# Gating the row loads of batches 2 and 3 to the MLP passes, five value blocks by crossbar, and a new order for batch 0, in a chunked-attention and MLP kernel

## The chip, the cores and the metric

One core of a Trainium2 chip runs the whole kernel. The metric is device time of one execution in microseconds (us), the median of several runs; lower is better. A profile is one further execution, taken by the hardware profiler, in which every instruction has a start and a duration.

The engines named below: TensorE (PE; PEld is its weight load, which overlaps), VectorE (DVE), ScalarE (ACT), GpSimd (POOL) and SyncE (SP). POOL and SP issue nearly all DMAs here. [...]

## The reference

Four batches, eight heads, 768 positions of 64 numbers. Attention goes by chunks of 32 queries; each chunk sees its own 32 positions, 16 to the left, 8 to the right, and 8 memory positions of its batch and head. The result of all heads becomes rows of 512, and each row goes through an MLP with a sine in it.

```python
for c in range(S // 32):
    l_start, r_end = max(0, 32 * c - 16), min(S, 32 * c + 32 + 8)
    k_full = concat([mem_k, k[:, :, l_start:r_end]], axis=2)
    v_full = concat([mem_v, v[:, :, l_start:r_end]], axis=2)
    a = softmax(q[:, :, 32 * c:32 * c + 32] @ k_full.T / sqrt(64))
    attn[:, :, 32 * c:32 * c + 32] = a @ v_full
x = attn.transpose(0, 2, 1, 3).reshape(4 * 768, 512)
h = x @ w_in                      # 512 -> 2048
g = h + sin(alpha * h) ** 2 / (alpha + 1e-9)
out = g @ w_out                   # 2048 -> 512, float32
```

Keys, queries, values and weights are cast to bf16 on the way in; sums are float32.

## The kernel before

The work is cut by batch. A batch has an attention part, a first MLP pass (`layer`: 16 tiles `ft` of 128 hidden columns, each two halves of four 384-column matmuls, L483) and a second MLP pass (`second`: six row blocks `s`, each 16 matmuls of 512 columns, L529, then a copy out of PSUM to `o_sb` and a store). The second pass of a batch is put into a `Feed` and dealt out in small shares between the instructions of the next batch's attention and first pass. So PE's order, written by hand, is: attention 0, first pass 0, second pass 0 mixed with turning K and Q of batch 1 and with attention 1, first pass 1, then attention 2 mixed with second pass, and so on; last comes second pass 3 alone.

Attention works on eight blocks `j` of 96 queries with 128 keys each (16 left, 48, 8 memory, 48, 8 right). `scores` (L270) makes the transposed scores of all heads, ACT takes three exponentials (L283), `values` (L296) multiplies by V with a column of ones, DVE normalizes (L302, L303) into `x_blk`, and the block is turned into `xT`, the operand of the first pass. There are two ways to turn it: `turn_x` (four PE transposes, L313, and a DVE copy, L316), or a crossbar DMA issued on SP (L467). The argument `crossed` of `attention` says how many of the eight blocks take the crossbar: 0 in batches 1 and 2, 5 in batch 3. `ahead` begins the first pass of a batch inside its attention, as soon as half of `xT` is there.

K and Q come in two ways. Batches 0 and 1 load them with many positions per partition (`load_qk`), and PE turns them (`turn`); for batch 1 POOL first puts two heads side by side (`pair_up`). Batches 2 and 3 load rows (`load_rows`, 22 POOL DMAs with rows of 64 numbers: 16 for `kst`, 6 for `qst`), and SP turns them by crossbar DMA into `kTs` and `qTs` (`cross_steps`, 14 DMAs). The rows of batch 2 are issued before attention 1, their crossings partly beside attention 1, the rest at tile 0 of first pass 1. The rows of batch 3 are issued at the end of first pass 1, and all 14 crossings come at tile 2 of first pass 2.

V is loaded by `load_v` into `vws` (two buffers, one for even and one for odd batches): per block 48 + 48 rows in the middle, and two more DMAs for the edges of 16 and 8 rows. Memory values go in by a DVE copy for batch 0 (`put_memv`) and by eight SP DMAs for the others (`send_memv`). V of batch 1 is issued at tile 11 of first pass 0, V of batches 2 and 3 after attention 1 and 2.

Each POOL or SP queue works in order, and a DMA's issue waits on its queue until its semaphores allow it. POOL's DMAs share eight completion semaphores in turn, so that the ninth waits for the first to land; SP's have eight as well. All stores of `o_sb` are on SP, with the crossings. `o_sb` has two buffers. In a first pass an even row block is copied out by DVE (L542) and an odd one by ACT (L544); in an attention (`state["attending"]`) all are copied by ACT.

Batch 0 has its own attention, by head pair `hp` and half: `unit_scores`, `unit_values`, `unit_turn`. PE's order in `attention_first` has dummy matmuls in it (`warm`, L323). All scores come first, then the eight `pv` (values) and `x` (turn) units.

PSUM banks are handed out from rings set by `plan`: `one` (single banks: turned blocks, second pass, warm), `big` (pairs: scores, values, the first pass begun ahead), `h` (pairs of the first pass), `t` (turned K and Q).

Of the kernel before, what the change touches and what calls it, by code (L numbers as in the profile page):

```python
# [42 lines left out]
def kernel(  # L43
# [37 lines left out]
    def plan(**sets):  # L81
        for kind, ring in sets.items():
            rings[kind] = list(ring)
# [37 lines left out]
    memkT = consts.tile([P, HP, 32], BF, name="memkT")  # L121
    w_in_sb = consts.tile([P, KT, d_ff], BF, name="w_in_sb")
    w_out_sb = consts.tile([P, FT, d_model], BF, name="w_out_sb")
    ident_f = consts.tile([FT, FT], F32, name="ident_f")
    alpha_sb = consts.tile([P, FT], F32, name="alpha_sb")
    inv_alpha = consts.tile([P, FT], F32, name="inv_alpha")
# [3 lines left out]
    def alloc_qk():  # L130
        kb = qkst.tile([P, H, 6, D], BF, name="k_bf")
        qb = qkst.tile([P, H, 6, D], BF, name="q_bf")
        return kb, qb

    def load_rows(b):
        for j in range(NJ):
            lo = QW * j - 16
            r0 = max(0, -lo)
            nc.gpsimd.dma_start(  # L139
                kst[r0:64, j, :].rearrange("p (h d) -> p h d", d=D),  # L140
                k[b, :, lo + r0:lo + 64, :].rearrange("h p d -> p h d"),
            )
            n = min(56, S - (QW * j + 48))
            nc.gpsimd.dma_start(  # L144
                kst[72:72 + n, j, :].rearrange("p (h d) -> p h d", d=D),
                k[b, :, QW * j + 48:QW * j + 48 + n, :].rearrange("h p d -> p h d"),
            )
        nc.sync.dma_start(
            kst[64:72], memk_st[64:72, b - 2, :].unsqueeze(1).to_broadcast([NM, NJ, H * D])
        )  # L150
        for t in range(NSUB):
            nc.gpsimd.dma_start(  # L152
                qst[:, t, :].rearrange("p (h d) -> p h d", d=D),
                q[b, :, P * t:P * t + P, :].rearrange("h p d -> p h d"),
            )

    def cross_steps(b):
        for j in range(NJ):
            nc.sync.dma_start_transpose(kTs[b % 2][:, :, P * j:P * j + P], kst[:, j, :])
            yield  # L160
        for t in range(NSUB):
            nc.sync.dma_start_transpose(qTs[b % 2][:, :, P * t:P * t + P], qst[:, t, :])  # L162
            yield

    def load_qk(b, bufs, h0, h1):
        for src, dst in ((k, bufs[0]), (q, bufs[1])):
# [4 lines left out]

    def load_v(b, parts=((0, H),)):
        vw = vws[b % 2][:].rearrange("p h j c -> p (h j) c")
        vf = v[b].rearrange("h (j t) d -> t (h j) d", t=QW)
        n = H * NJ
        if len(parts) > 1:
            load_v_edges(vw, vf, n)
        for h0, h1 in parts:
            c0, c1 = h0 * NJ, h1 * NJ
            nc.gpsimd.dma_start(vw[16:64, c0:c1, 0:D], vf[0:48, c0:c1])  # L180
            nc.gpsimd.dma_start(vw[72:120, c0:c1, 0:D], vf[48:96, c0:c1])
        if len(parts) == 1:
            load_v_edges(vw, vf, n)

    def load_v_edges(vw, vf, n):
        nc.gpsimd.dma_start(vw[0:16, 1:n, 0:D], vf[80:96, 0:n - 1])
        nc.gpsimd.dma_start(vw[120:128, 0:n - 1, 0:D], vf[0:8, 1:n])

    def put_memv(b, eng, h0, h1):
        eng.tensor_copy(  # L190
# [188 lines left out]
    def attention_first(kq, alphas, ahead):  # L379
# [3 lines left out]
        def turn_k(hp):  # L383
            t = turn(kq[0], hp, None)
            put_k(0, hp, t)
            put_k_edges(0, hp, t)

        def turn_q(hp):
            put_q(0, hp, turn(kq[1], hp, None))

        def sc(hp):
            for half in range(2):
                pt[hp, half] = unit_scores(hp, half)

        def pv(*u):
            xb[u] = unit_values(*u, pt[u])
# [11 lines left out]
        put_memk(0)  # L408
        warm(3)
        turn_k(1)  # L410
        warm(2)
        sc(0)
        turn_q(1)
        alphas()
        put_memv(0, nc.vector, 0, H)
        warm(2)
        turn_k(2)
        warm(2)
        sc(1)
        turn_q(2)  # L420
        turn_k(3)
        warm(4)
        turn_q(3)
        sc(2)
        warm(2)
        sc(3)
        nc.scalar.preload_act_table(ACTF.Sin)
        send_memv(1)
        plan(big=(4, 0, 2), one=(6, 7))
        units = [(hp, half) for hp in range(HP - 1) for half in range(2)]  # L430
        pv(0, 0)
        for n in range(1, len(units)):
            warm(1)
            pv(*units[n])
            warm(1)
            x(*units[n - 1])
        warm(1)
        pv(3, 0)
        x(2, 1)
# [80 lines left out]
    def second(i, gT, cut=0):  # L520
# [15 lines left out]
        def end_o(s, bank):  # L536
            kept.remove(bank)
            rings["one"].remove(bank)
            rings["one"].append(bank)
            o_sb = mlp.tile([P, d_model], F32, name="o_sb", bufs=2)  # L540
            if s % 2 == 0 and not state["attending"]:
                nc.vector.tensor_copy(o_sb[:], ps[:, bank, :])  # L542
            else:
                nc.scalar.copy(o_sb[:], ps[:, bank, :])  # L544
            nc.sync.dma_start(out[S * i + P * s:S * i + P * s + P, :], o_sb[:])
# [26 lines left out]
        nc.vector.memset(vw[96:128, H - 1, NJ - 1, 0:D], 0.0)  # L572
    load_qk(0, kq, 0, 2)
    masks.make_identity(nc, ident[:])
    for hp in range(1, HP):
        load_qk(0, kq, 2 * hp, 2 * hp + 2)
    load_v(0, [(2 * hp, 2 * hp + 2) for hp in range(HP)])
    nc.gpsimd.dma_start(memv_st[64:72, 1:B].rearrange("n b h d -> n (b h) d"),
                        mem_v[1:B].rearrange("b h n d -> n (b h) d"))
    for kT in kTs:  # L580
        nc.vector.memset(kT[:, :, 0:16], 0.0)
        nc.vector.memset(kT[:, :, 848:856], 0.0)
# [37 lines left out]
    xT = attention_first(kq, alphas, ahead)  # L620
    for c in range(2):
        load_w_out(c)
    kq1 = alloc_qk()
    load_qk(1, kq1, 0, H)
    for bb in range(2):
# [29 lines left out]
    def begin_0(ft):  # L655
        if ft == 3:
            plan(h=[6] + rings["big"])
        if ft == 11:
            load_v(1)
        if ft == 15:  # L660
            prs.extend(pair_up(kq1[0], n) for n in range(3))

    layer(0, xT, "VPPAPAVPPAPAVAAA", begin_0, 0)
    last4 = rings["h"]
# [2 lines left out]
    feed.take(20)  # L667
    for pc in range(2 * HP):
        hp = pc % HP
        if pc + 3 < 2 * HP:  # L670
            prs.append(pair_up(kq1[(pc + 3) // HP], (pc + 3) % HP))
        t = turn(None, hp, prs[pc])
        if pc < HP:
            put_k(1, hp, t)
            put_k_edges(1, hp, t)
        else:
            put_q(1, hp, t, hp % 2 == 1)
        feed.take(2)
    nc.scalar.preload_act_table(ACTF.Exp)
    feed.take(4)  # L680
    load_rows(2)
    crossings = cross_steps(2)
    xT = attention(1, feed, (6, 8, 4, 4, 4, 3, 3, 3, 3, 1, 1), 2, 0, crossings, 3)
    load_v(2)
    send_memv(2)

    for i in range(1, B):
        last = i == B - 1
        if i > 1:
            crossings = cross_steps(i + 1) if not last else iter(())  # L690

        def begin(ft, i=i):
            if ft == (2 if i > 1 else 0):
                for _ in crossings:
                    pass

        if i == 1:
            assert feed.left() == 16
# [5 lines left out]
            plan(h=rings["big"])  # L704
            layer(i, xT, "AAAV", begin, feed.left() - (0 if last else 16))
        if not last:
            if i + 2 < B:
                load_rows(i + 2)
            plan(big=rings["h"])
            nc.scalar.preload_act_table(ACTF.Exp)  # L710
            feed.take(6)
            xT = attention(i + 1, feed, (4, 8, 4, 4, 3, 3, 3, 3, 4, 4, 4), 2, 5 if i == B - 2 else 0)
            if i + 2 < B:
                load_v(i + 2)
                send_memv(i + 2)
    feed.take(200)


# [28 lines left out]
```

The softmax here doesn't subtract the row's maximum and nothing guards it: scores larger than these inputs give would overflow.

## Time and profile before

Three runs took 225.8 to 226.97 us, the median is 226.94. The profiled execution took 227.97 us; its span from the first to the last instruction is 226.2 us, so 1.8 us lie around the span.

| Stage (us of the span) | What PE does |
|---|---|
| 0 to 5.6 | warm-up, while the first K lands |
| 5.6 to 29.1 | attention 0, and the first pass begun ahead |
| 29.1 to 49.2 | first pass 0 |
| 49.2 to 61.3 | K and Q of batch 1 turned, second pass 0 |
| 61.3 to 78.3 | attention 1 with second pass 0 |
| 78.3 to 99.7 | first pass 1 |
| 99.7 to 118.9 | attention 2 with second passes 0 and 1 |
| 118.9 to 149.7 | first pass 2 with second pass 1 |
| 149.7 to 168.0 | attention 3 with second passes 1 and 2 |
| 168.0 to 226.2 | first pass 3, second passes 2 and 3 |

Views used in this document: the page (busy time of each engine, DMA queues, groups by line), a table of stages, the waits of an engine, the chain of work that ended last, the timeline of an engine, and the DMA view of a stretch. In a row of a timeline stand the start, the duration, the engine, the line, the operation and the count; a bracket gives the idle time before it and who ended it.

### The profile page before, as it was taken

To read this page: it belongs to the slowest core of one execution; us is meant where nothing else is said; L and a number is where in the kernel's file an instruction comes from. 1 tells how busy PE (TensorE), PEld (TensorE's weight loads), DVE (VectorE), ACT (ScalarE), POOL (GpSimd) and SP (SyncE) were. 2 spreads that over 40 slices of the span, in tenths; PEclk is the share of its full clock that TensorE was granted. 3 is DMA by queue.
4 is the path that set the end of the run, shared out by engine and by line. 5 is a ranking of instruction groups with operands and counts; after the bars stand their busy time and mean duration, and the time that the engine had idled before them with its cause. 6 is when DMAs were issued, how large, how long until landed. Compare 5 with 4: busy or idle time off the path is not lost.

```text
span 226.2 us, 4432 instructions
## 1 busy us (share of the span) xinstructions
PE 212.5 (94%) x1694; PEld 115.9 (51%) x1720; DVE 132.9 (59%) x234; ACT 152.6 (67%) x226; POOL 84.4 (37%) x106
## 2 busy tenths in 40 slices
PE   7998999999998999999999999978999999999992
PEld 2555555555545655554665555534565555544440
DVE  5684748793516769994763875626653773771110
ACT  2558478894787589999756879777939678651011
POOL 8967843796989941185780000000000000000000
PEclk9999999999999999999999999999999999999999
DMA  5999999999999999999999954542330110111211
GB/s 81 174 121 127 157 210 207 206 204 142 103 216 159 142 112 167 117 135 121 151 180 95 96 95 93 96 139 93 73 110 0 49 46 0 48 48 49 93 65 74
DMA packets 94573, 25.97 MB, mean 115 GB/s; under 512 B 82632, under 2 KB 91480, under 8 KB 94552
## 3 DMA queue, kind: packets, MB, share of 16 engines
q0 software_dynamic: 71520, 14.81, 111.5%
q1 hardware_dynamic: 23032, 10.88, 24.5%
q8 instruction: 13, 0.21, 0.5%
q14 instruction: 8, 0.07, 0.1%
HBM read 29.67 MB, written 6.29 MB: 159 GB/s over the span
## 4 chain that ended last, share of the span: by engine, by line
PE 50%; DVE 7%; ACT 4%; SPq 3%; issue 3%; DMA 1%; DVEq 0%; ACTq 0%
PE ps L529 26%; PE ps L483 18%; DVE gT L513 5%; SPq L162 3%; PE ps L296 2%; PE ps L270 2%; DVE u L510 2%; ACT u L503 2%; PE ps L313 1%; ACT u L507 1%; DMA out_dram<-o_sb 1%; ACT o_sb L544 1%; ACT pt L283 0%; DVE o_sb L542 0%; DVEq L513 0%
## 5 line engine op out<-in xcount | busy, mean ns | idle before, releaser
L529 PE MATMUL ps<-w_out_sb,gT 128*128 128x512 bf16 x362 | 94.7, 379 | 1.5 <-ACT o_sb L544 0.4
L483 PE MATMUL ps<-xT,w_in_sb 128*128 128x384 bf16 x512 | 91.2, 326 | 1.6 <-DVE gT L513 1.2
L513 DVE SCALAR_TENSOR_TENSOR gT<-u,inv_alpha,ps 128x768 bf16<-128x768 f32 x64 | 63.3, 1011 | 24.0 <-ACT u L507 20.0
L483 PEld LDWEIGHTS <-w_in_sb 128*128 128x128 bf16 x512 | 49.6, 98 | 39.0 <-issue 3.4
L503 ACT ACTIVATE u<-ps,alpha_sb 128x768 f32<-128x768 f32 x64 | 56.7, 896 | 18.4 <-PE ps L483 17.5
L529 PEld LDWEIGHTS <-gT 128*128 128x128 bf16 x384 | 34.3, 98 | 30.9 <-issue 0.9
L507 ACT ACTIVATE u<-u 128x768 f32<-128x768 f32 x40 | 33.7, 843 | 1.2
L283 ACT ACTIVATE pt<-ps,biasm 128x256 bf16<-128x256 f32 x72 | 28.6, 481 | 6.7 <-PE ps L270 3.2
L544 ACT COPY o_sb<-ps 128x512 f32<-128x512 f32 x16 | 9.4, 589 | 25.5 <-PE ps L529 25.5
L510 DVE TENSOR_TENSOR u<-u 128x768 f32<-128x768 f32 x18 | 17.1, 953 | 6.0 <-ACT u L503 6.0
L542 DVE COPY o_sb<-ps 128x512 f32<-128x512 f32 x8 | 5.5, 690 | 21.8 <-PE ps L529 17.2
L303 DVE TENSOR_TENSOR x_blk<-ps,rinv 96x512 bf16<-96x512 f32 x24 | 16.5, 686 | 0.8
L144 POOL DMA_DIRECT2D kst<-in_k_dram x16 | 11.6, 725 | 8.8 <-DMA vw<-in_v_dram 4.1
L302 DVE RECIPROCAL rinv<-ps 96x8 f32<-96x8 f32 x24 | 4.9, 202 | 17.0 <-ACT pt L283 10.7
L139 POOL DMA_DIRECT2D kst<-in_k_dram x16 | 11.0, 689 | 8.6 <-DMA vw<-in_v_dram 6.2
L323 PE MATMUL ps<-idle 128*128 128x512 bf16 x35 | 12.5, 448 | 1.5 <-DVE vw L571 1.2
L249 ACT COPY kT<-ps 128x672 bf16<-128x672 bf16 x8 | 5.8, 719 | 9.5 <-PE ps L234 6.7
L296 PEld LDWEIGHTS <-pt 128*128 128x128 bf16 x192 | 9.0, 98 | 4.6 <-issue 0.7
L510 POOL TENSOR_TENSOR u<-u 128x768 f32<-128x768 f32 x6 | 8.9, 1495 | 6.1 <-ACT u L503 6.1
L152 POOL DMA_DIRECT2D qst<-in_q_dram x12 | 10.6, 899 | 1.2 <-DMA kst<-in_k_dram 1.2
L270 PE MATMUL ps<-qT,kT 64*128 64x96 bf16 x192 | 8.3, 205 | 2.6 <-DVE gT L513 2.3
L296 PE MATMUL ps<-vw,pt 128*128 128x65 bf16 x192 | 9.8, 193 | 0.4 <-issue 0.3
(77 smaller groups left out, 150.8 us busy)
## 6 DMA issues: line engine op xcount, KB each, us to landing
out_dram<-o_sb SPq DMA_DIRECT2D x24, 256.0 KB
vw<-in_v_dram POOLq DMA_DIRECT2D x6, 384.0 KB, 14.9
w_out_sb<-in_moe_w_out_dram POOLq DMA_DIRECT2D x2, 1024.0 KB, 18.8
w_in_sb<-in_moe_w_in_dram POOLq DMA_DIRECT2D x3, 512.0 KB, 10.1
qst<-in_q_dram POOLq DMA_DIRECT2D x12, 128.0 KB, 7.0
kst<-in_k_dram POOLq DMA_DIRECT2D x14, 64.0 KB, 6.7
kst<-in_k_dram POOLq DMA_DIRECT2D x14, 56.0 KB, 6.4
k_bf<-in_k_dram POOLq DMA_DIRECT2D x4, 192.0 KB, 4.7
```

What stands on the lines that cost most here:

```text
L270: nc.tensor.matmul(sc[:, e, QW * hp:QW * hp + QW], kTs[b % 2][64 * e:64 * e + 64, hp, pitch * j:pitch * j + P], qTs[b % 2][64 * e:64 * e + ...
L283: nc.scalar.activation(pt[:, 0:H * QW].rearrange("p (g e c) -> p g e c", g=2, e=4)[:, :, :, 32 * m:32 * m + 32], sc[:, :, 0:4 * QW].rearra ...
L296: nc.tensor.matmul(otv[:, e, hp, :], pt[:, QW * i:QW * i + P], vws[b % 2][:, 2 * hp + e, j, 0:D + 1],)
L303: nc.vector.tensor_tensor(out=x_blk[:].rearrange("p g e d -> p e g d"), in0=otv[0:QW, :, :, 0:D], in1=rinv[:].unsqueeze(3).to_broadcast([Q ...
L323: nc.tensor.matmul(z, idle[:, 0:P], idle[:])
L483: nc.tensor.matmul(hT[:, hf, 0:HALF], w_in_sb[:, kt, P * ft:P * ft + P], xT[:, kt, HALF * hf:HALF * hf + HALF], start=(kt == 0), stop=(kt ...
L503: nc.scalar.activation(u[:], hT[:, :, 0:HALF], ACTF.Sin, scale=alpha_sb[:, ft:ft + 1])
L507: nc.scalar.activation(u[:], u[:], ACTF.Square)
L510: eng.tensor_tensor(out=u[:], in0=u[:], in1=u[:], op=ALU.mult)
L513: nc.vector.scalar_tensor_tensor(out=gT[:, ft, :].rearrange("p (e c) -> p e c", e=2), in0=u[:], scalar=inv_alpha[:, ft:ft + 1], in1=hT[:, ...
L529: nc.tensor.matmul(ps[:, bank, :], gT[:, ft, P * s:P * s + P], w_out_sb[:, ft, :], start=(ft == 0), stop=(ft == FT - 1),)
L544: nc.scalar.copy(o_sb[:], ps[:, bank, :])
```

## The change

Six things are changed.

- **Row loads.** `load_rows` issues K and Q in the order in which the blocks need them (`order`), and the crossings take the same order. The rows of batch 2 are issued at tile 0 of first pass 1, those of batch 3 at tile 0 of first pass 2. Ahead of each set POOL copies one element of `xT`, the last that attention writes, into `gate`, so that the loads behind it on POOL start when that attention is over. The crossings of batch 2 are all issued at tile 0 of first pass 1, those of batch 3 one per tile from tile 1 of first pass 2.
- **V loads.** `load_v` takes the edges along: 64 + 56 rows per block in two DMAs. V of batches 1 and 2 and both `send_memv` go at tile 11 of first pass 0; V of batch 3 follows the rows of batch 3, `send_memv(3)` attention 2.
- **Crossbar.** Attention 1 and 2 send five value blocks through the crossbar, as attention 3 did already.
- **Copies out.** In an attention all `o_sb` copies go to DVE.
- **Batch 0.** V of the first head pair is issued ahead of K and Q of pairs 2 and 3; `put_memv` is earlier; three values units and two turns are placed between the scores. Eight dummy matmuls fewer are issued.
- **Batch 1.** Four head pairs are paired up at tile 15 instead of three, and later ones after the turn instead of before it. The memory values' load is behind the loads of `w_out`.

```diff
+    order = ((0, 0), (1, 1), (2, 2), (3,), (4, 3), (5, 4), (6, 5), (7,))
     def load_rows(b):
-        for j in range(NJ):
+        for jt in order:
+            j = jt[0]
...
+            for t in jt[1:]:
+                nc.gpsimd.dma_start(qst[:, t, :]..., q[b, :, P * t:P * t + P, :]...)
...
     def load_v(b, parts=((0, H),)):
...
+            if b == 0 and h0 == 0:
+                part(16, 64, 0, 0, 1)
+                c0 = 1
+            part(0, 64, -16, c0, c1)
...
+            part(72, 128, 48, c0, c1)
...
         turn_k(1)
+        put_memv(0, nc.vector, 0, H)
         warm(2)
         sc(0)
         turn_q(1)
         alphas()
-        put_memv(0, nc.vector, 0, H)
-        warm(2)
-        turn_k(2)
-        warm(2)
+        warm(3)
         sc(1)
+        t2 = turn(kq[0], 2, None)
+        put_k(0, 2, t2)
+        pv(0, 0)
+        put_k_edges(0, 2, t2)
         turn_q(2)
-        turn_k(3)
-        warm(4)
+        warm(1)
+        pv(0, 1)
+        t3 = turn(kq[0], 3, None)
+        put_k(0, 3, t3)
+        warm(1)
+        x(0, 0)
+        sc_half(2, 0)
+        put_k_edges(0, 3, t3)
         turn_q(3)
-        sc(2)
-        warm(2)
+        sc_half(2, 1)
+        x(0, 1)
+        warm(1)
+        plan(big=(4, 0, 2))
+        pv(1, 0)
         sc(3)
...
-            if s % 2 == 0 and not state["attending"]:
+            if s % 2 == 0 or state["attending"]:
...
         if ft == 11:
             load_v(1)
+            load_v(2)
+            send_memv(1)
+            send_memv(2)
...
-    load_rows(2)
-    crossings = cross_steps(2)
-    xT = attention(1, feed, (6, 8, 4, 4, 4, 3, 3, 3, 3, 1, 1), 2, 0, crossings, 3)
-    load_v(2)
-    send_memv(2)
+    xT = attention(1, feed, (6, 8, 4, 4, 4, 3, 3, 3, 3, 1, 1), 2, 5)
...
         def begin(ft, i=i):
-            if ft == (2 if i > 1 else 0):
+            if i == 1 and ft == 0:
+                nc.gpsimd.tensor_copy(gate[:], xT[0:1, 0, S - 1:S])
+                load_rows(2)
                 for _ in crossings:
                     pass
+            if i == 2:
+                if ft == 0:
+                    nc.gpsimd.tensor_copy(gate[:], xT[0:1, 0, S - 1:S])
+                    load_rows(3)
+                    load_v(3)
+                if ft >= 1:
+                    next(crossings, None)
...
-            xT = attention(i + 1, feed, (4, 8, 4, 4, 3, 3, 3, 3, 4, 4, 4), 2, 5 if i == B - 2 else 0)
-            if i + 2 < B:
-                load_v(i + 2)
-                send_memv(i + 2)
+            xT = attention(i + 1, feed, (4, 8, 4, 4, 3, 3, 3, 3, 4, 4, 4), 2, 5)
+            if i == 1:
+                send_memv(3)
```

## The prediction

> **What bounds the kernel now.** I read the busy times first, then the table of stages, the waits of PE, the chain that ended last, SP's timeline and the DMA view, in that order.
>
> ```profile
> PE 212.5 (94%) x1694; PEld 115.9 (51%) x1720; DVE 132.9 (59%) x234; ACT 152.6 (67%) x226; POOL 84.4 (37%) x106
> ```
>
> PE is busy for 212.5 of 226.2 us, so it is the bound: only 13.7 us are idle. Time is won by taking work off PE or by closing its few gaps. The stages (span, PE, PEld, DVE, ACT and POOL busy, clock, DMA share, GB/s):
>
> ```profile
> 5.60:29.10 23.50, 21.97 (x315) 12.67 (x319) 15.24 (x43) 14.03 (x21) 18.62 (x24) 1.00 2.20 147
> 61.30:78.30 17.00, 15.98 (x204) 9.43 (x208) 8.89 (x23) 12.76 (x28) 15.78 (x21) 1.00 1.92 169
> 78.30:99.70 21.40, 20.39 (x126) 11.79 (x124) 18.38 (x21) 19.51 (x24) 7.62 (x11) 1.00 2.28 132
> 99.70:118.90 19.20, 18.29 (x215) 10.52 (x219) 12.63 (x27) 15.09 (x32) 14.45 (x18) 1.00 2.40 150
> 118.90:149.70 30.80, 30.59 (x171) 16.67 (x172) 17.71 (x19) 25.30 (x30) 0.00 (x0) 1.00 1.50 95
> 149.70:168.00 18.30, 15.94 (x186) 8.46 (x189) 11.24 (x22) 12.78 (x29) 0.00 (x0) 1.00 0.32 100
> ```
>
> The clock is full throughout. First pass 2 leaves PE no gap; attention 3 loses 2.4 us. PE's waits, and the chain around the longest, say why:
>
> ```profile
> PE ps L270 <- DVE gT L513: 2.3, 2, 2.0
> PE ps L313 <- ACT o_sb L544: 0.6, 1, 0.6
> PE ps L529 <- ACT o_sb L544: 0.4, 1, 0.4
> ...
> 147.82 1.22 SPq L162
> 149.03 0.04 issue
> 149.08 0.02 SPq L545
> 149.10 0.03 issue
> 149.13 2.23 DMA out_dram<-o_sb
> 151.35 0.03 issue
> 151.38 0.02 DVEq L542
> 151.40 0.04 issue
> 151.44 0.69 DVE o_sb L542
> 152.14 0.93 DVE gT L513
> ```
>
> SP issues 14 crossings without a break; a store stands behind them, both `o_sb` buffers are taken, DVE waits 4.6 us for one, the last `gT` waits behind that copy, and PE stands still for 2.05 us at 151. The other two waits are PE at a bank that ACT has not copied out. Last, the DMA queues from 91 to 101 us, where six crossings run beside the row loads (q0 is POOL's queue, q1 SP's):
>
> ```profile
> DMA packets 8762, 1.24 MB, mean 124 GB/s; under 512 B 8762, under 2 KB 8762, under 8 KB 8762
> q0 software_dynamic: 6449, 0.73, 215.5%
> q1 hardware_dynamic: 2313, 0.51, 52.6%
> ```
>
> POOL's loads ran at 645 packets/us there; the engines were busy in every slice from 5.7 to 120 us.
>
> [...] the loads slow down beside crossings (645 packets/us, against 7154 in the 8.6 us from 11 to 19.6, 832/us, with none). [...] every crossing here lies on the queue of the stores; in the trace each takes about 1.22 us of SP. [...] the 2.05 us gap left it at 1.00.
>
> **Part by part.** Times are of the profiled execution: span 226.2, run 227.97, which is 1.03 above the median of 226.94. I take the differences from the median.
>
> *Batch 0 (gain 1.9).* Before, DVE idles until V lands at 19.5 and then needs 0.85 to 0.9 us for each of eight values units (0.20 + 0.69); the stage ends at 29.1 with the third half begun ahead. After, I walk the new order with the rows' durations: exp 0.76, K copy 0.72, edges 0.32, Q copy 0.95, x copy 0.48, on PE a turn of a pair 0.45, half of a score 0.70, values 0.24. PE does the first values unit at 13.5, when pair 1's scores are done. DVE then runs on end: unit (0,0) to 14.6, edges 15.0, Q2 15.9, unit (0,1) 16.8, edges 17.1, Q3 18.1. Values (1,0) take the banks that Q3 leaves, at 18.1; pair 3's exponentials end at 20.6, the Sin table load at 21.9, the copy of x(1,0) at 22.35. A warm matmul waits for that copy's bank, so PE idles 1.1 us: the table load, hidden before, is not now. Then units (2,1), (3,0) end on DVE at 23.75 and 24.8, x(3,0) is copied at 25.5, and the stage ends at 27.2. PE agrees: eight warms less are 8 × 0.214 = 1.7.
>
> Inputs: K2 issues at 7.1 instead of 4.8 and lands 4.7 later, 11.8; needed at 13.0. Q3: 9.2 + 5.1 = 14.3, needed 16.4. V of pair 0 is issued by 7.1 and needed at 13.5; its landing took 9.2 behind twelve loads, here it has four before it. I take 6, on time; at 9.2 PE is 2.8 late and the gain is gone. Bounds: 2.8 (no table stall) to -0.9. `w_in` is issued earlier and needed 1.7 earlier; slack stays. Q of batch 1 lands at 53.4, its pairs end 0.83 apart from 54.3, PE's turns move to 55.1 and on at 0.77: 0.7 of slack left. POOL issues four V loads (5.4 us) instead of 4.3 ahead of the pairs; K lands at 49.1 anyhow.
>
> *Crossbar and copies (gain 1.05 and 0.75).* Five blocks less turned on PE: 5 × 4 transposes at 0.043 = 0.85 per attention, plus the `o_sb` gaps of 0.61 (attention 1) and 0.38 (attention 2) as DVE now copies (0.69 each; its idle time covers it). Attention 3, crossed already, confirms the size: from its second score to the third half ahead 153.11 to 168.32 = 15.2, attention 2 102.58 to 118.85 = 16.3. Less: the last copy at 78.4 now goes ahead of the last turn on DVE (0.3), and crossings lie behind V of batch 2 in the DMA engines in attention 1. The fourth block is ready near 69.5, issued to 70.7, needed at 73.1. The trace has no landing time of a crossing; from attention 3, where the fourth, issued by 163.3, is used at 165.97 without a gap, it is at most 2.7; I take 2.7 for free engines and 0.4 more as a charge. The 0.3 stands by itself in the sum. In attention 2 SP may still be at row crossings, below: 0.5.
>
> *Rows of batch 2 (0 to 4, in the 0.5).* The gate itself is below 0.3 (POOL's smallest memset 0.09); 22 loads queue behind it, nothing else. They start at T1 = 78.9 of before's time, the end of attention 1's last copy. Issue: 16 × 0.71 + 6 × 0.89 = 16.7. Packets: 120 rows a block less 16, times 8 heads, plus 768 × 8: 13,696. At 645/us 21.2; landed by T1 + 23, the last crossing done near T1 + 28. The last score needs it at 112.6, T1 + 33.7; the first value block's crossing, behind on SP, is ready at T1 + 28. Just met.
>
> *Stores of batch 2's pass (gain 2.05).* Crossings come one per tile, stores between them at tiles 5 and 10: no third buffer is needed before the first is stored. The gap goes.
>
> *Rows and V of batch 3 (loss 1.0).* Now late: V follows the rows behind the gate. They start at T2 = 119.5, where attention 2's last copy ended before. 13,696 + 7,656 packets at 645/us are 33.1, plus 1.7 of start and landing: T2 + 34.8. Needed by the first values, 155.94 less the 2.05 gap: T2 + 34.4. That is 0.4 late; with a tail for the last load I take 1.0. Below: at 832/us, T2 + 27.4, nothing. Above: at 559, T2 + 39.9, 5.5; this is the rate of before's last stretch of loads, 11 K loads of some 480 packets, 6 Q of 1,024 and one V, 19,100 in all, from 97.6 to 131.8 (the last V issue at 116.93 and its 14.9 to landing).
>
> Sum: -1.9 - 1.05 - 0.75 - 2.05 + 1.0 + 0.3 = -4.45, so 226.94 - 4.45 = 222.5 (profiled run 223.5).
>
> **The rivals.** *Everything hides (0.17):* no V wait, no charge for late crossings, 1.9 + 1.46 + 1.23 + 2.05 = 6.64: 220.3. For it: the V edges of 8 and 16 rows are gone, and from 11 to 19.6 us small packets went at 832/us. Against: behind T2 the loads share the engines with 14 crossings, 8 memory sends and the stores.
>
> *Batch 0's gain fails (0.17):* V of pair 0 lands 9.2 after issue, -0.9 for 1.9: 225.3; with the bank wait longer, about 226.
>
> *Slower (0.20): V of batch 3 late in earnest.* Eight semaphores, each held for a load's landing: at 9.6 us (rows took up to 10.8 for Q, 19 for K) a load issues each 1.2 us, 22 take 26.4, V's issue 2.7, its landing 15 (medians 13.0 to 17.6): T2 + 44.3, PE waits 9.9. 226.94 - 6.64 + 9.9 = 230.2. It decides from T2 + 42.2, 7.8 late. For it: POOL's waits at 83 to 98 with five loads of up to 5.0 us. Against: those stood behind V loads, these do not.
>
> **Numbers.** Forecast 222.5 with 0.46 (221 to 224.7). A measurement can tell about 0.5%, 1.1 us, from no change. Faster by more: 0.46 + 0.17 + 0.03 = 0.66; within: 0.14; slower: 0.20. The range 220.0 to 229.5 leaves out half of the slower case and a little below.
>
> **What would show it.** Right: the third half begun ahead ends near 27.2 with one PE gap near 21 to 22; L313 falls by 40 matmuls; DVE's 4.6 us wait for a store is gone; in attention 3 the first L296 waits for V by 0 to 2 us. Wrong: a first L355 waiting for V at 13.5; L270 waiting for crossings in attention 2; L483 waiting for `xT` crossings; L296 of batch 3 waiting over 5 us.

## The result, and the profile after

The kernel after took 238.36 us (median of 4 runs, 237.44 to 239.62) against 226.45 us for the kernel before, run beside it. The ratio is 1.053, with a 95% interval of 1.047 to 1.059: 11.9 us slower. The forecast was 222.5 us. A ratio leaves out executions more than 1.5% above the fastest of their kernel, so it need not equal the ratio of the two medians. The profiled execution has a span of 237.0 us in a run of 238.74 us, 10.8 us above the profiled execution of before, so the two profiles can be laid side by side.

The first page of the kernel after, busy times first, then the slices of the granted clock:

```profile
PE 214.0 (90%) x1647; PEld 114.9 (48%) x1672; DVE 135.8 (57%) x233; ACT 148.1 (62%) x217; POOL 82.8 (35%) x102
...
PEclk9999999997699999999999999997799999999999
```

PE is busy for 1.5 us more than before, with 47 instructions fewer, and its idle time grew from 13.7 to 23.0 us. Two stretches show a clock below full speed, which the kernel before has nowhere. PE's waits, longest first (the columns are the total in us, the times it occurred, and the longest):

```profile
PE ps L244 <- POOL pr L235: 5.6, 1, 5.6
PE ps L309 <- issue: 5.2, 1, 5.2
...
PE ps L336 <- ACT xT L388: 1.0, 1, 1.0
PE ps L507 <- DMA xT<-x_blk: 0.5, 1, 0.5
```

Two single waits, with a low clock behind each, carry the loss. L244 is the first turn of K of batch 1, which waits for a pair that POOL puts together (`pair_up`, L235). L309 is `values` in attention 3, which waits for V of batch 3; the profile names only "issue" because the load that releases it is not tied to the instruction.

By stages (span, then busy time and count of PE, PEld, DVE, ACT and POOL, the clock, the DMA share, GB/s), first the turns of batch 1 with the second pass, then attention 1, 2 and 3:

```profile
48.20:68.40 20.20, 14.23 (x87) 7.88 (x87) 6.80 (x16) 7.75 (x11) 9.06 (x10) 0.83 2.75 129
68.40:84.40 16.00, 15.23 (x185) 8.13 (x189) 8.86 (x20) 11.80 (x26) 0.00 (x0) 1.00 0.26 67
106.10:124.10 18.00, 17.54 (x195) 9.08 (x199) 13.36 (x25) 13.90 (x29) 0.00 (x0) 1.00 0.64 110
155.00:178.70 23.70, 18.02 (x190) 9.17 (x193) 11.90 (x24) 11.25 (x26) 0.00 (x0) 0.86 0.77 107
```

The first and the last row are the two with a low clock, 0.83 and 0.86. The landmarks of PE's timeline divide the difference of the two spans as follows. Each stage runs to the same instruction in both kernels.

| Stage | before, us | after, us | difference |
|---|---|---|---|
| to the first pass begun ahead in attention 0 | 29.1 | 28.2 | -0.9 |
| first pass 0, K and Q of batch 1 turned, to scores of batch 1 | 32.2 | 40.2 | +8.0 |
| attention 1 | 17.0 | 16.0 | -1.0 |
| first pass 1 | 22.7 | 23.1 | +0.4 |
| attention 2 | 17.8 | 16.6 | -1.2 |
| first pass 2 | 30.9 | 30.9 | 0.0 |
| attention 3 | 18.6 | 23.8 | +5.2 |
| the rest | 57.9 | 58.3 | +0.4 |

So attentions 0, 1 and 2 did become shorter, by 3.1 us together, and two stages lost 13.2.

The first loss starts on POOL. Its timeline (start, duration, operation, count; in brackets the idle time before and what ended it):

```profile
42.88 1.47 POOL L534 TENSOR_TENSOR u<-u 128x768 f32<-128x768 f32 x1 [1.21 <-ACT u L527]
44.28 4.99 POOL L183 DMA_DIRECT2D vw<-in_v_dram  x3
55.81 1.69 POOL L183 DMA_DIRECT2D vw<-in_v_dram  x1 [6.54 <-issue]
57.49 3.13 POOL L235 COPY pr<-k_bf 128x768 bf16<-128x768 bf16 x4
```

Three V loads are issued without a break, then POOL stands still for 6.54 us ahead of the fourth. The four pair copies behind it, whose data (K of batch 1, issued at 23.52 and landed 22.0 later) were there since 45.5, start at 57.49. VectorE had no work from 51.9 to the end of that wait, so it is not what held POOL. In the kernel before the four smaller V loads went out without a break, and the pairs followed at 49.44:

```profile
48.63 0.82 POOL L187 DMA_DIRECT2D vw<-in_v_dram  x1
49.44 3.12 POOL L222 COPY pr<-k_bf 128x768 bf16<-128x768 bf16 x4
```

On PE of the kernel after this gives:

```profile
49.65 3.18 PE L553 MATMUL ps<-w_out_sb,gT 128*128 128x512 bf16 x14
58.39 0.82 PE L244 MATMUL ps<-ident,pr 128*128 128x128 bf16 x6 [5.55 <-POOL pr L235]
59.00 1.06 PE L553 MATMUL ps<-w_out_sb,gT 128*128 128x512 bf16 x2
...
63.92 0.50 PE L244 MATMUL ps<-ident,pr 128*128 128x128 bf16 x6
64.26 0.59 PE L553 MATMUL ps<-w_out_sb,gT 128*128 128x512 bf16 x2
```

After 5.55 us of idling the same two groups take 0.82 and 1.06 us; from 63.9 on, 0.50 and 0.59. That is the low clock: between 58 and 61 us the granted clock is 0.50. The second loss looks the same on PE, ahead of the first values of attention 3:

```profile
158.59 0.61 PE L553 MATMUL ps<-w_out_sb,gT 128*128 128x512 bf16 x2
164.42 0.60 PE L309 MATMUL ps<-vw,pt 128*128 128x65 bf16 x8 [5.22 <-issue]
```

V of batch 3 was issued behind the gated row loads. The gate opened at 124.78; the two large V loads were issued at 142.36 and 144.0 and landed 12.2 and 20.3 us later, the second at 164.3, which is when PE goes on:

```profile
124.78 0.18 POOL L724 COPY gate<-xT 1x1 bf16<-1x1 bf16 x1 [22.32 <-DVE xT L329]
142.36 3.35 POOL L183 DMA_DIRECT2D vw<-in_v_dram  x2 [0.50 <-issue]
```

In between the page gives the DMA engines 9 tenths or more in every slice from 124.4 to 165.9. From 124.8 to 164.5, the two queues and the second large V load:

```profile
q0 software_dynamic: 22656, 2.73, 116.5%
q1 hardware_dynamic: 8914, 3.16, 51.1%
...
vw<-in_v_dram POOLq DMA_DIRECT2D x1, 441.0 KB, 20.3
```

POOL's queue (q0) moved 22,656 packets; from the first row load at 125.3 to 164.3 that is 581 per us. This count is more than that of the rows loaded: in the trace 21,304 of these packets have 128 bytes and 1,352 have 4.

### The profile page after: what moved, and what is told of

Same layout as the page of the kernel before. It is cut to its first block, busy times and chain, and to the rows that moved or that the text cites. A ratio compares the mean times of both kernels' runs of the same rounds, so it can differ in the third digit from the quotient of the medians.

```text
span 237.0 us, 4354 instructions
## 1 busy us (share of the span) xinstructions
PE 214.0 (90%) x1647; PEld 114.9 (48%) x1672; DVE 135.8 (57%) x233; ACT 148.1 (62%) x217; POOL 82.8 (35%) x102
## 4 chain that ended last, share of the span: by engine, by line
PE 59%; DVE 7%; issue 4%; ACT 3%; DMA 1%; DVEq 0%; ACTq 0%
PE ps L553 32%; PE ps L507 20%; DVE gT L537 3%; PE ps L283 3%; PE ps L309 2%; DVE u L534 2%; ACT u L527 2%; PE ps L244 1%; DMA xT<-x_blk 1%; PE ps L326 1%; DVE o_sb L566 1%; ACT u L531 1%; ACT pt L296 1%; DVE qT L269 0%; ACT kT L262 0%
## 5 line engine op out<-in xcount | busy, mean ns | idle before, releaser
L553 PE MATMUL ps<-w_out_sb,gT 128*128 128x512 bf16 x362 | 97.4, 388 | 1.2 <-DVE gT L537 0.2
L507 PE MATMUL ps<-xT,w_in_sb 128*128 128x384 bf16 x512 | 91.3, 326 | 2.3 <-DVE gT L537 1.3
L507 PEld LDWEIGHTS <-w_in_sb 128*128 128x128 bf16 x512 | 49.5, 98 | 40.0 <-issue 4.9
L553 PEld LDWEIGHTS <-gT 128*128 128x128 bf16 x384 | 34.8, 99 | 31.5 <-issue 0.9
L566 DVE COPY o_sb<-ps 128x512 f32<-128x512 f32 x17 | 11.7, 689 | 25.3 <-PE ps L553 24.7
L183 POOL DMA_DIRECT2D vw<-in_v_dram x15 | 18.1, 1212 | 7.0 <-issue 7.0
L316 DVE TENSOR_TENSOR x_blk<-ps,rinv 96x512 bf16<-96x512 f32 x24 | 16.5, 686 | 1.0 <-DVE rinv L315 0.3
L568 ACT COPY o_sb<-ps 128x512 f32<-128x512 f32 x7 | 4.1, 584 | 19.0 <-PE ps L553 19.0
L309 PE MATMUL ps<-vw,pt 128*128 128x65 bf16 x192 | 10.2, 197 | 5.2 <-issue 5.2
L309 PEld LDWEIGHTS <-pt 128*128 128x128 bf16 x192 | 9.4, 101 | 10.1 <-issue 6.5
L315 DVE RECIPROCAL rinv<-ps 96x8 f32<-96x8 f32 x24 | 4.8, 202 | 15.6 <-PE ps L309 11.7
L336 PE MATMUL ps<-idle 128*128 128x512 bf16 x28 | 10.1, 471 | 2.3 <-DVE vw L595 1.2
L143 POOL DMA_DIRECT2D kst<-in_k_dram x16 | 11.1, 692 | 0.6 <-issue 0.4
L153 POOL DMA_DIRECT2D qst<-in_q_dram x12 | 10.8, 900 | 0.1
## 6 DMA issues: line engine op xcount, KB each, us to landing
vw<-in_v_dram POOLq DMA_DIRECT2D x3, 512.0 KB, 12.2
vw<-in_v_dram POOLq DMA_DIRECT2D x2, 448.0 KB, 11.9
```

Of the source, the lines that this page charges most:

```text
L183: nc.gpsimd.dma_start(vw[p0:p1, c0:c1, 0:D], flat[r0:r0 + QW * (c1 - c0)].rearrange("(n t) d -> t n d", t=QW)[0:p1 - p0],)
L309: nc.tensor.matmul(otv[:, e, hp, :], pt[:, QW * i:QW * i + P], vws[b % 2][:, 2 * hp + e, j, 0:D + 1],)
L316: nc.vector.tensor_tensor(out=x_blk[:].rearrange("p g e d -> p e g d"), in0=otv[0:QW, :, :, 0:D], in1=rinv[:].unsqueeze(3).to_broadcast([Q ...
L507: nc.tensor.matmul(hT[:, hf, 0:HALF], w_in_sb[:, kt, P * ft:P * ft + P], xT[:, kt, HALF * hf:HALF * hf + HALF], start=(kt == 0), stop=(kt ...
L553: nc.tensor.matmul(ps[:, bank, :], gT[:, ft, P * s:P * s + P], w_out_sb[:, ft, :], start=(ft == 0), stop=(ft == FT - 1),)
```

## The experiments

Where an attention's length is given below, it runs from its first scores to the end of the first half tile begun ahead: before, 16.0, 16.1 and 16.9 us for attentions 1, 2 and 3. Runs are set against the kernel before on the same chip. Where one run is named, it is a single execution of the kernel, and a difference below 1 us is not read from it.

**V of batch 2 behind the pairs.** One of the two suspected waits is taken away.

```diff
         if ft == 11:
             load_v(1)
-            load_v(2)
...
         feed.take(2)
+    load_v(2)
     nc.scalar.preload_act_table(ACTF.Exp)
```

> V of batch 2 is issued behind the eight pair copies of batch 1 instead of ahead of them; nothing else differs from the changed kernel. If its second load, which POOL issued only at 55.8 us, is what holds the pair copies, PE's wait of 5.55 us before the first turn of K goes, and with it the slow stretch behind it (four turn steps of 1.47 us instead of 0.77, 2.6 us): about 8 us less, 230. If the pairs are late because K and Q of batch 1 land late, the wait stays and the time stays at 238.

Measured: 231.34 us, ratio 1.025 (1.020 to 1.030), so 7 us of the loss are gone. The wait at L244 is gone, the one at L309 is 4.9. POOL in this kernel:

```profile
45.06 3.36 POOL L183 DMA_DIRECT2D vw<-in_v_dram  x2
48.42 3.15 POOL L235 COPY pr<-k_bf 128x768 bf16<-128x768 bf16 x4
```

The pairs start right behind two V loads. The loss of the turns is V of batch 2, standing ahead of the pairs on POOL.

**Fewer rows of V ahead of the pairs.** What holds the fourth load? V of batch 2 stays at tile 11, but in two loads of 48 partitions; the edges of 16 and 8 rows come behind the pairs. `load_v_rows` issues one load for each triple: from partition, to partition, first position.

```diff
             load_v(1)
-            load_v(2)
+            load_v_rows(2, ((16, 64, 0), (72, 120, 48)))
...
         feed.take(2)
+    load_v_rows(2, ((0, 16, -16), (120, 128, 96)))
```

> V of batch 2 stays where it is, with two loads still, but each takes 48 partitions instead of 64 and 56; its edges come behind the pair copies. If POOL's wait of 6.5 us before the second load comes from too many rows being outstanding (4096 + 3584 + 4096 before it; now 3072 for the third and fourth), the wait shrinks to under 1 us, the pairs begin near 49.5 us, and the time is about 230. If it is a wait for one of POOL's DMA semaphores or for a count of loads, four large loads are still outstanding and the 6.5 us stay.

Measured in one run: 229.25 us. POOL issues all four without a break:

```profile
44.22 3.36 POOL L193 DMA_DIRECT2D vw<-in_v_dram  x2
47.57 2.66 POOL L182 DMA_DIRECT2D vw<-in_v_dram  x2
50.23 3.12 POOL L245 COPY pr<-k_bf 128x768 bf16<-128x768 bf16 x4
```

The number of loads is the same as in the kernel after; what is smaller is the number of their packets. A load of 64 rows of 64 blocks is 4,096 packets, one of 56 is 3,584, one of 48 is 3,072: 13,824 in the four loads here, 15,360 there. In the trace of the kernel after POOL's queue moved 15,488 packets of 128 bytes from 44.28 to 70 us, these 15,360 and 128 for two loads of memory keys of 8 KB each. V of batch 3 was late by 3.5 us here, and in this profile that wait is put down to the load itself:

```profile
PE ps L319 <- DMA vw<-in_v_dram: 3.5, 1, 3.5
```

**Three quarters of the last load.** If the number of packets makes the wait, a size between should wait for less. The fourth load takes 48 of its 64 blocks (2,688 packets, 14,464 in all), the rest goes behind the pairs.

```diff
-            part(72, 128, 48, c0, c1)
+            if low == "rest":
+                c0 = 48
+            part(72, 128, 48, c0, 48 if low == "most" else c1)
...
-            load_v(2)
+            load_v(2, low="most")
...
         feed.take(2)
+    load_v(2, low="rest")
```

> The fourth V load at tile 11 takes 48 of its 64 columns (2688 rows instead of 3584), the other 896 rows follow behind the pair copies. Outstanding rows would be 14464 instead of 15360. [...] the wait before that load is below 1 us and the time is about 230. If the limit is lower, or is not on rows, 5 to 6.5 us of wait stay.

Measured in one run: 234.77 us; the wait at V of batch 3 was 7.2 us in this execution, so the time, 230 in the expectation, says little. POOL says more:

```profile
44.22 4.98 POOL L185 DMA_DIRECT2D vw<-in_v_dram  x3
51.01 1.42 POOL L185 DMA_DIRECT2D vw<-in_v_dram  x1 [1.81 <-issue]
```

The wait is 1.81 us instead of 6.54, neither below 1 nor the 5 to 6.5 that were expected, and it ends 0.4 us after Q of batch 1 landed (issued at 24.75, 25.9 to landing: 50.65). In the kernel after Q landed at 50.1 and did not end the wait; the first V load, issued at 44.28 with 11.1 to landing, landed at 55.4, 0.4 before POOL went on. So with 13,824, 14,464 and 15,360 packets, in four loads each time, POOL waited 0, 1.81 and 6.54 us: the wait grows with the packets, and the count of loads does not set it. Bytes do not set it either: in the run with fewer rows the fourth load started at 48.9 with 2,496 KB not yet landed (Q and three V loads, and itself), and in the kernel after it was still held when these were 1,920 KB, from 50.1 to 55.4. That the packets hold POOL is inferred from these three sizes; what it waited for, no view shows.

**TensorE kept warm through the wait.** Is the slow clock part of the price? Twenty-four dummy matmuls are put ahead of the first turn; POOL is left as it is.

```diff
     for pc in range(2 * HP):
         hp = pc % HP
+        if pc == 0:
+            for _ in range(24):
+                nc.tensor.matmul(ps[:, rings["t"][0], :], idle[:, 0:P], idle[:])
         t = turn(None, hp, prs[pc])
```

> 24 dummy matmuls (5.1 us) are put on PE ahead of the first turn of K of batch 1, where PE waited for 5.55 us; everything else is the changed kernel, so the pairs come as late as before. If the turn steps behind the wait were slow because the clock had dropped in the gap, they go back to 0.77 us each and the time falls by about 2.6 us, to 235.7. If they were slow because the pair copies pace them, they stay at 1.47 us and the time stays at 238.

Measured in one run: 235.87 us, 2.5 below the kernel after, as expected. POOL still waits:

```profile
55.93 1.69 POOL L183 DMA_DIRECT2D vw<-in_v_dram  x1 [6.67 <-issue]
```

```profile
52.66 5.34 PE L701 MATMUL ps<-idle 128*128 128x512 bf16 x24
58.50 0.51 PE L244 MATMUL ps<-ident,pr 128*128 128x128 bf16 x6 [0.51 <-POOL pr L235]
```

PE idles for 0.5 us where it idled for 5.55, the groups of turns take 0.51 us, as they do at the full clock in the kernel after (0.49 to 0.50), and scores of batch 1 begin at 66.32 instead of 68.44. So about 2.1 to 2.5 us of the first loss are the clock after the wait, on top of the wait.

**The second gate left out.** The gate of batch 3 delays the rows and V of batch 3; without it they start when POOL is free.

```diff
                 if ft == 0:
-                    nc.gpsimd.tensor_copy(gate[:], xT[0:1, 0, S - 1:S])
                     load_rows(3)
```

> The one-element copy ahead of the rows of batch 3 is left out; the loads keep their place in POOL's order, so they start when the rows of batch 2 are issued, near 102 us, instead of 125. If the 5.2 us wait of attention 3 is V of batch 3 landing behind the gated rows, V lands before 150 us, the wait and the slow steps behind it (about 2 us) go, and the time is about 231. If V is late because the DMA engines cannot carry rows, V and crossings in any case, or if the earlier rows now hold up the crossings of batch 2, attention 2 or 3 still waits and the gain is below 3 us.

Measured: 236.8 us, ratio 1.043 (1.036 to 1.050). V of batch 3 is on time, but:

```profile
PE ps L244 <- POOL pr L235: 4.9, 1, 4.9
PE ps L507 <- DMA xT<-x_blk: 3.3, 1, 3.3
```

The rows now run beside attention 2, and the crossbar turns of its value blocks are late, by 3.3 us for the first pass. One wait was exchanged for another, with the clock at 0.63 from 124 to 128 us, around the end of that wait.

**V of batch 3 moved, gates kept.** The load goes right behind the rows of batch 2, alone and then together with the first move.

```diff
                 load_rows(2)
+                load_v(3)
...
                     load_rows(3)
-                    load_v(3)
```

> Only V of batch 3 is moved, right behind the rows of batch 2; V of batch 2 stays at tile 11. The wait before the first turn of K and its slow steps stay (8 us), the wait of attention 3 goes with its slow steps: about 231. If V of batch 3 is not the cause of that wait, 238.

Measured in one run: 235.59 us, not 231; waits of 5.2 us at L244 and of 3.6 at L507.

With V of batch 2 behind the pairs as well:

> V of batch 2 behind the pair copies, and V of batch 3 right behind the rows of batch 2, in the stretch from 103 to 124 us in which the DMA engines were at 2 to 5 tenths; both gates stay. If the two V loads account for the loss, both PE waits (5.6 and 5.2 us) and the slow steps behind them are gone, and what is left is the gain of the other parts: 231.3 less about 7, 224.5, some 0.8% below the kernel before. If V of batch 3 now delays the last crossings of batch 2 or the crossings of attention 2, part comes back as a wait of L507 for xT, as without the gate, and the time is 226 to 228.

Measured: 227.95 us, ratio 1.004 (1.001 to 1.006): the rival's range. Both waits of the kernel after are gone, and one new one stands on PE at the end of attention 2:

```profile
113.73 0.59 PE L553 MATMUL ps<-w_out_sb,gT 128*128 128x512 bf16 x2
117.81 0.81 PE L507 MATMUL ps<-xT,w_in_sb 128*128 128x384 bf16 x4 [3.49 <-DMA xT<-x_blk]
```

The profiled execution took 229.15 us, 1.2 above the median. The half tile begun ahead reads blocks 0 to 3, so PE waits for the fourth crossing. The trace has the times at which the semaphore of each of SP's DMAs was raised, which no view prints; the last of them is the landing. The fourth crossing's issue ended at 111.72, it landed 6.0 us later, at 117.68, and PE went on at 117.81. With V of batch 2 moved alone, when no V load ran there, the same crossing landed 2.9 us after its issue (111.57, 114.50), and PE waited for it for 0.2 us. Beside POOL's loads the five crossings landed 4.8 to 7.3 us after the ends of their issues, without them 1.1 to 2.9. The clock is 0.69 from 117 to 121.

**Turn on TensorE where loads run.** The same kernel, with attention 2 turning all its value blocks on TensorE.

```diff
-            xT = attention(i + 1, feed, (4, 8, 4, 4, 3, 3, 3, 3, 4, 4, 4), 2, 5)
+            xT = attention(i + 1, feed, (4, 8, 4, 4, 3, 3, 3, 3, 4, 4, 4), 2, 0 if i == 1 else 5)
```

> As both_v_moved (V of batch 2 behind the pairs, V of batch 3 right behind the row loads of batch 2, both gates kept), but attention 2 turns all eight value blocks on TensorE. Theory (a crossbar turn is late only because loads of POOL are in flight beside it, and TensorE's clock drops in that wait): the 3.5 us wait of the first MLP pass for xT goes, the clock in the 31 us behind it rises from 0.94 to 1.00 (about 1.8 us), 20 TensorE turns come back (about 1.2 us): 227.95 - 3.5 - 1.8 + 1.2, about 224, ratio to before 0.990. Rival (the V of batch 3 in flight beside attention 2 holds up something else too, such as the crossings of batch 2 or the stores): a new wait of 2 us or more in attention 2 or behind it, and 226 to 228.

Measured: 225.39 us, ratio 0.9945 (0.9927 to 0.9963). No wait over 1.2 us is left and the clock is full. Removing the crossbar from attention 2 is worth 2.6 us by the medians and 2.1 by the ratios, where 4 were expected. The wait for `xT` and the low clock behind it are gone, as the theory has it.

**No gates at all, with and without crossbar.** What are the gates for?

```diff
             if i == 1 and ft == 0:
-                nc.gpsimd.tensor_copy(gate[:], xT[0:1, 0, S - 1:S])
                 load_rows(2)
...
                 if ft == 0:
-                    nc.gpsimd.tensor_copy(gate[:], xT[0:1, 0, S - 1:S])
                     load_rows(3)
```

V of batch 2 is behind the pairs in both. With five crossed blocks in attentions 1 and 2:

> V of batch 2 behind the pairs, and both gate copies left out. Theory (the gates are there for the crossbar turns alone): V of batch 3 is in time, no wait before attention 3's values, but the pass behind attention 1 and the pass behind attention 2 each wait 3 to 4 us for xT, with slow clock behind it: 228 to 231. Rival (the gates are not needed at all once the value loads are out of the way): no wait of more than 1 us for xT and about 224.

Measured: 233.8 us, ratio 1.033 (1.028 to 1.037), slower than expected by 3. The waits:

```profile
PE ps L507 <- DMA xT<-x_blk: 8.0, 3, 5.7
```

They are 5.66 us in attention 1, and 0.2 and 2.14 in attention 2. With none crossed in attentions 1 and 2:

> As no_gates, but attentions 1 and 2 turn all their value blocks on TensorE (attention 3 keeps its five by crossbar, as the kernel before has). Theory: both waits for xT go, 40 TensorE turns come back (about 2.3 us against the kernel after); 225 to 226, close to the kernel before with batch 0's part alone (ratio 0.996). Rival (the row loads beside attentions 1 and 2 cost by more than the crossbar): waits of 2 us or more elsewhere, 228 or more.

Measured: 226.1 us, ratio 1.000 (0.998 to 1.002), and no wait over 1.2 us. So the gates serve the crossbar turns and nothing else that these runs show: with the crossbar they save waits in attentions 1 and 2, without it they are not needed.

**Three blocks instead of five.** Is a crossing late by a fixed time, or until the loads have drained?

```diff
-            xT = attention(i + 1, feed, (4, 8, 4, 4, 3, 3, 3, 3, 4, 4, 4), 2, 0 if i == 1 else 5)
+            xT = attention(i + 1, feed, (4, 8, 4, 4, 3, 3, 3, 3, 4, 4, 4), 2, 3 if i == 1 else 5)
```

> As moved_no_crossbar_2, but attention 2 turns three value blocks by crossbar instead of none (both_v_moved had five and waited 3.5 us). The third block's values come about 3.8 us before the fifth's. Theory (a crossing beside loads is late by a fixed 3 to 4 us behind its own issue): no wait over 0.5 us for xT, 12 TensorE turns fewer: about 0.7 us less than moved_no_crossbar_2, 224.7, ratio 0.991. Rival (the crossings are late until the V loads have drained, at about 117 us, whatever their number): a wait of 2 us or more for xT in the first MLP pass and 226.5 to 228.

Measured: 225.39 us, ratio 0.9958 (0.9940 to 0.9975). PE waits 0.3 us for a crossing, as the theory of a fixed time expects, but the landings do not bear that theory out. The three crossings landed at 114.10, 114.53 and 114.74, that is 6.6, 5.7 and 4.6 us after their issues had ended, and the last V load at 114.32. So the lateness is not a fixed time, and the rival is not excluded: the loads ended here 2.7 us before the 117 that it took, and the short wait does not tell the two apart. Against a wait for the end of all loads stands the kernel without gates: in its attention 1 crossings landed 6.2 to 7.3 us after their issues, from 75.9 on, while rows went on landing until 91.2. What exactly a crossing waits for stays open. Attention 2 was 15.6 us instead of 16.5 in the profile, but the median shows no gain from it.

**Batch 0's part alone**, put on the kernel before: the new order in `attention_first`, V with its edges, the order of the loads of batch 0.

```diff
-    load_v(0, [(2 * hp, 2 * hp + 2) for hp in range(HP)])
+    load_v0(0, ((0, 2),))
...
+    load_v0(0, ((2, 4), (4, 6), (6, 8)))
...
+        pv(0, 0)
...
         turn_q(2)
```

> The kernel before with batch 0's part of the change alone: V of batch 0 with its edges, V of the first pair ahead of K and Q of pairs 2 and 3, and the new order in the first attention. In the changed kernel's profile that attention ended 0.9 us earlier than before, 1.0 us of table load uncovered. If that part stands by itself, 0.9 us less than the kernel before (0.996); if the start is eaten up by Q of batch 1 landing when it did, no difference.

Measured: 225.67 us, ratio 0.996 (0.995 to 0.998), a gain of 0.9 us.

**The same with the output copies on VectorE.**

```diff
-            if s % 2 == 0 and not state["attending"]:
+            if s % 2 == 0 or state["attending"]:
```

> The kernel before with batch 0's part and with the output copies of the attention stages on VectorE instead of in turn. Attention 1 and attention 2 were 1.0 and 1.24 us shorter in the kernel after. Theory A (that came from ScalarE's relief by the copies): about 2 us less than batch 0's part alone, ratio to before 0.988. Theory B (it came from the 40 TensorE turns and the ScalarE/VectorE copies of turned blocks that the crossbar took over): no more than 0.3 us from it, ratio 0.995 to 0.997. Against both: VectorE is late with the reciprocals, ratio above 0.997.

Measured: 226.78 us, ratio 1.002 (1.001 to 1.004), 1.1 us more than without. Attention 1 was 15.5 us, attention 2 16.3. The copies gain half a microsecond in attention 1 and nothing in attention 2, and lose it elsewhere.

**The copies as before, in the repaired kernel.** This is `moved_no_crossbar_2` with that one line put back.

```diff
-            if s % 2 == 0 or state["attending"]:
+            if s % 2 == 0 and not state["attending"]:
```

> As moved_no_crossbar_2 (225.39, ratio 0.9945), with the output copies in turn on VectorE and ScalarE in the attention stages too, as the kernel before has them. Theory B (the copies on VectorE gain nothing, as the run of batch 0's part with them was 1.1 us slower than without): 224.3, ratio 0.990, and attention 2 (scores to the first half tile ahead) back from 16.5 to 16.1 us, attention 1 no longer than 14.9. Theory A (within the changed order the copies pay): 226 or more and attention 1 at 15.0 or more.

Measured: 223.65 us, ratio 0.987 (0.984 to 0.990), the fastest of all: both V loads moved, the crossbar in attentions 1 and 3 only, copies as in the kernel before (even blocks on VectorE outside attention, the rest on ScalarE), batch 0's part kept. Its stages, attention 1, 2 and 3, to the second half tile begun ahead:

```profile
60.88:76.10 15.22, 15.22 (x185) 7.97 (x185) 7.51 (x18) 12.58 (x28) 0.00 (x0) 1.00 1.51 159
99.05:116.40 17.35, 16.76 (x208) 9.76 (x208) 11.36 (x26) 13.74 (x30) 0.00 (x0) 1.00 1.49 131
147.74:163.80 16.06, 16.00 (x188) 8.30 (x188) 10.05 (x21) 12.71 (x29) 0.00 (x0) 1.00 0.38 89
```

PE has no idle time to speak of in attentions 1 and 3. Attention 1 is 14.4 us, with the crossbar and the old copies, 1.6 less than in the kernel before, so the copies are not needed for the gain there. What is left is the crossbar together with the row loads of batch 2, which no longer run beside attention 1; no run takes these two apart.

## Why the prediction was wrong

*Four V loads ahead of the pairs (+8.0, priced at nothing): the step that failed most.* The prediction put it as "POOL issues four V loads (5.4 us) instead of 4.3 ahead of the pairs; K lands at 49.1 anyhow". The issue was priced as if a load were issued whenever the engine came to it. The fourth one was held for 6.5 us, PE waited 5.55 us, and the slow clock took 2.1 to 2.5 us more, together about what the stage lost. Moving V of batch 2 took 7 us off.

*V of batch 3 behind the rows (+1.0 predicted, a 5.2 us wait measured).* The mechanism, the place and the need were right: PE was ready for V at T2 + 34.4, as predicted, with T2 now at 124.8. V landed at T2 + 39.5, close to the upper end of T2 + 39.9. The term that was mis-sized is the time of the packets: 33.1 us predicted, 39.0 measured, for two reasons. First, the prediction divided the rows it had counted, 21,352, by a rate read off the view, which counts other packets too. The view has 22,656 packets for these loads; at 645 per us they take 35.1 us. Second, the rate was 581 and not 645: 645 came from a stretch in which six crossings ran; here 14 crossings, memory sends and stores (8,914 packets of SP) ran in the same stretch. The lower rate is the other 3.9 us. The bound of 559 had been worked out from rows and time; in rows the rate here was 546. The named slower case was this wait in earnest, 9.9 us, 230.2 us. Its place was right and its mechanism was not: no semaphore held the 22 row loads, which were issued without a break from 125.3 to 141.9. In the kernel before one did hold a load: a K load of POOL stood 5.02 us, to 91.57, and went out 0.3 us after the V load eight before it on POOL, issued at 75.37, had landed at 91.28. Alone it could not reach 238.

*The clock (no term at all).* The prediction says of the clock only that the 2.05 us gap of the kernel before left it at 1.00, and gave none of its waits a price for it, its rival of 9.9 us neither. In the runs the clock was at 0.50 right behind gaps of 5.55 and 5.22 us, at 0.69 from 117 to 121 us around the end of the gap of 3.49 us (both V loads moved), and at 0.63 from 124 to 128 us around the end of that of 3.26 us (second gate left out). One gap of 2.14 us was also followed by a low clock, of 0.58. In attention 3 the price is the same as in the turns: it took 22.1 us, and 14.5 to 14.8 in the kernels above whose V came in time, 7.3 to 7.6 more for a wait of 5.2. Each of the two waits over 5 us thus cost its length and then 2.1 to 2.5 us.

*Batch 0 (1.9 predicted, 0.9 measured).* The table load laid bare was predicted as a PE gap of 1.1 us; it was 0.98, and the load itself took 1.28 us on ScalarE. V was on time. What failed is "DVE then runs on end": behind Q3 it waited for PE's values time and again.

```profile
18.99 0.20 DVE L374 RECIPROCAL rinv<-ps 96x8 f32<-96x8 f32 x1 [0.48 <-PE ps L368]
19.23 0.69 DVE L375 TENSOR_TENSOR x_blk<-ps,rinv 96x512 bf16<-96x512 f32 x1
20.64 0.20 DVE L374 RECIPROCAL rinv<-ps 96x8 f32<-96x8 f32 x1 [0.73 <-PE ps L368]
...
23.68 0.20 DVE L374 RECIPROCAL rinv<-ps 96x8 f32<-96x8 f32 x1 [1.18 <-PE ps L368]
```

In these rows of the kernel after, VectorE idles for 0.48, 0.73 and 1.18 us ahead of single values units, each time for PE; the stage ended at 28.2 instead of 27.2.

*Crossbar and copies (1.05 and 0.75 predicted, 1.0 and 1.24 measured).* About right in sum, wrong in part: the gain of the attentions does not need the copies, and the copies on VectorE cost 1.1 to 1.7 us over the whole kernel (225.67 to 226.78 on the kernel before, 223.65 to 225.39 on the repaired one). Where outside the attentions they lose it was not traced to a wait.

*The store gap (2.05 predicted).* The gap is not in the kernel after, as predicted. But it was in one profiled execution, and was taken from the median of all: the kernel with batch 0's part alone, which leaves stores and crossings of before as they were, has attention 3 at 14.8 us, without the gap, against 16.9 in that execution. This suggests that in the median the term was worth little. It is not shown: only one execution of the kernel before was profiled, and batch 0's part shifts what follows by 0.6 us, which may close the gap by itself.

*Row crossings, gate, pass 1 (0.5).* The gate copy took 0.18 us, predicted below 0.3; PE's waits show none for a crossing of K or Q. The last copy at the end of attention 1 (0.3) is not seen as a wait of its own.

## What to carry to other kernels

A load moved ahead of other work on its issuing queue has to be priced with everything that is already outstanding on that queue, and not by its issue time: it may stand in the queue, as the fourth V load did for 6.54 us here, and what stands behind it stands too. Where transfers compete, forecast a landing from the rate of a stretch with the same mixture of traffic, with packets and rate counted in the same way, and carry the bad end of the range into the decision when the thing that waits is the bound engine. Crossbar turns landed 4.6 to 7.3 us after the ends of their issues beside V loads here and 1.1 to 2.9 without them, so give each attention the turn that suits the traffic beside it. Price a wait of TensorE of some 5 us, when it is the bound engine, at its length and 2.1 to 2.5 us, as the waits of 5.55 and 5.22 us cost here; behind gaps of 2.14 to 3.49 us the clock was low too, but what that cost was not measured by itself.

## What the runs showed of the hardware

- POOL stood still ahead of the fourth of four loads with 15,360 packets together, for 6.54 us; with 14,464 in four loads for 1.81 us, until 0.4 us after Q had landed; with 13,824 not at all.
- The low clock lasted some 5 us after a wait of 5.55 us: it was 0.50 in every us from 57 to 63 and 1.00 from 64 to 70, and groups of six turns took 0.81 to 0.85 us from 58.39 to 62.84, and 0.50 from 63.92. A gap of 2.14 us (no gates, ending at 126.8) was also followed by a clock of 0.58 between 128 and 132 us; the gap of 2.05 us of the kernel before was not (1.00 from 150 to 156).
- A crossbar turn of a value block landed 4.6 to 7.3 us after the end of its issue beside V loads from POOL in attention 2. When POOL had no load in flight, in attentions 1 to 3 of the kernel after, 12 of 15 landed 1.1 to 1.2 us after it, the others 1.5, 2.6 and 2.7.
